# Fifteen small transfers of x between two K blocks of a decode kernel

## The chip, the cores and the metric

The kernel runs on one core of a Trainium2 chip. A core has a matrix engine (TensorE, PE in the profile, with its weight loads as PEld), a vector engine (VectorE, DVE), an activation engine (ScalarE, ACT), a general engine (GpSimd, POOL) and a synchronising engine (SyncE, SP), which here issues transfers. Sixteen DMA engines move data between HBM and the core's memory SBUF. The metric is the device time in microseconds, lower is better; a profile is taken of one execution and gives its span from the first to the last instruction.

## The reference

One token is decoded. x is one row of 1024 numbers. It is normalised, and two branches start from the result xn:

```
x = A_x
xn = layernorm(x)
out = x + A(xn, k_cache, v_cache, wq, wo) + B(xn, w1, w2, w3, w4)

A: q = xn @ wq                      # 32 query heads of 128
   scores = q . k * 128**-0.5       # 4 key/value heads, 8 query heads on each
   o = softmax(scores) . v          # 65536 cached positions
   return o @ wo
B: h = gelu(layernorm(xn) @ w1)     # w1, w2 are 1024 x 1024
   x1 = xn + shifted(h) @ w2        # four quarters of h, shifted by +1, -1, +2, -2
   return x1 + gelu(layernorm(x1) @ w3) @ w4      # w3 1024 x 3584, w4 3584 x 1024
```

All arrays are bf16. The K and V caches hold 4 heads x 65536 positions x 128 numbers each, 67 MB each; with the weights some 170 MB are read for one row of output.

## The kernel before

One large SBUF tile, KV, has 98304 bf16 columns on all 128 partitions. It holds two K slots of 16384 columns (4 MB each, offsets KOFF) and two V slots of 32768 columns (8 MB each, offsets VOFF), and later the weights. KV is the last tile to be declared; a tile "align" of 96 columns stands before it and is used by nothing.

The main loop goes over 32 blocks n of 8192 positions, eight for each key/value head. A K load brings two blocks, a V load brings four. For a block, VectorE transposes K in place (Ttr, L501), PE computes the scores (QK, L511), VectorE and PE find the running minimum (stats1, MB, stats2), ScalarE takes the exponential (EXP, L539), PE and VectorE transpose the probabilities (PTr, L547 and L549), PE multiplies them with V (PV, L557), and ScalarE and GpSimd add the result to the running sum (FLASH, L565 to L570). The transposition and the scores of the next block are worked on while this one is finished.

Each engine has a list of its own (class _Q) that it goes through in the order written. A transfer is added with _dma: first the waits for earlier readers and writers of its target (_deps), then the issue, whose end raises the semaphore of its channel by 16. SP's list is straight: all loads of wq, K, V and the later weights, then the store of the result. At the end of iteration n come

```
            if n % 2:
                issue_k((n + 3) // 2)
            if n % 4 == 1:
                issue_v((n + 3) // 4)
```

so after iteration 17 SP issues K load 10 (L341; it waits until QK of blocks 16 and 17 has read the slot) and V load 5 (L349), and the next thing on its list is K load 11, after iteration 19, which waits for QK of block 19. K load 11 is read by the transposition of block 22. SP has one queue; what it issues is carried out by the DMA engines in that order. ScalarE issues one transfer, the load of x at the start (L329), on a queue of its own.

After the loop come the weights of branch B, wo and w4. The last of w4 arrives in four parts, its products are added into OUT_ps (L460), VectorE copies them (L717), SP stores them as four rows (L718) and waits for that store (L719).

Of the kernel before, what the change touches and what calls it, by code (L numbers as in the profile page):

```python
# [6 lines left out]
BF = mybir.dt.bfloat16  # L7
# [113 lines left out]
def _deps(q, reads, writes):  # L121
    need = {}
    for b in reads:
        for s, v in b.w.items():
            need[s] = max(v, need.get(s, 0))
    for b in writes:

        for s, v in (list(b.r.items()) if b.r and b.whole else list(b.w.items()) + list(b.r.items())):
            if not (q.in_order and s is q.sem):
                need[s] = max(v, need.get(s, 0))  # L130
    for s, v in need.items():
        q.wait((s, v))


def _done(ev, reads, writes, partial=False):
    for b in reads:
        b.add_read(ev)
    for b in writes:
        if partial:
            b.add_write(ev)  # L140
        else:
            b.set_write(ev)


def _op(q, fn, reads=(), writes=(), partial=False, tick=True):
    _deps(q, reads, writes)
    ev = q.op(fn, tick)
    _done(ev, reads, writes, partial)
    return ev
# [17 lines left out]
def _dma(q, chan, fn, reads=(), writes=(), partial=False):  # L167
    _deps(q, reads, writes)
    chan.n += 1
    ev = q.dma(fn, chan.sem, 16 * chan.n)  # L170
    _done(ev, reads, writes, partial)
    return ev


def bass_parallel_sum__gqa_block_cached__mixer_s_mlp__decode_kernel(
# [13 lines left out]
    P = 128  # L189
# [18 lines left out]
    with ExitStack() as es:  # L208
        E = es.enter_context

        def sb(name, shape, dt):
            return E(nc.sbuf_tensor(name, shape, dt))
# [4 lines left out]
        def sem(name):  # L217
            return E(nc.semaphore(name))
# [42 lines left out]
        acc = sb("acc", [P, KT_D], F32)  # L261
        g_bf = sb("g_bf", [P, KT_D], BF)
        gh_bf = sb("gh_bf", [P, KT_F], BF)
        sb("align", [P, 96], BF)
        KV = sb("KV", [P, 98304], BF)
        KOFF, VOFF = (0, 16384), (32768, 65536)
        EPI = KV[:, 61440:65536].bitcast(F32)
# [24 lines left out]
        q_sp = _Q("sp", None)  # L292
# [5 lines left out]
        def chan(name):  # L298
            if name not in chans:
                chans[name] = _DmaChan(sem("d_" + name))  # L300
            return chans[name]
# [41 lines left out]
        def issue_v(j):  # L343
            if j >= NV:
                return
            h, nb = divmod(j, NV // HKV)
            src = A_v_cache[0, h, nb * 4 * SUB:(nb + 1) * 4 * SUB, :].rearrange("(p c) d -> p (c d)", p=P)
            sl = j % 2
            _dma(q_sp, chan("v%d" % sl), lambda e: e.dma_start(out=KV[:, VOFF[sl]:VOFF[sl] + 32768], in_=src), writes=[b_V[sl]])  # L349
# [142 lines left out]
        def Ttr(n, idx):  # L492
            if n >= NT:
                for ix in idx:
                    q_dve.op(lambda e, ix=ix: e.memset(spare[:, ix:ix + 1], 0.0))
                return
            s, half = (n // 2) % 2, n % 2
            for ix in idx:
                c = KOFF[s] // 2 + 4096 * half + 1024 * ix
                _deps(q_dve, [b_K[s][half]], [])  # L500
                ev = q_dve.op(lambda e, c=c: e.transpose(out=KV32[:, c:c + 1024], in_=KV32[:, c:c + 1024]))  # L501
                b_T[s][half].add_write(ev)

        def QK(n):
            s, half = (n // 2) % 2, n % 2
            fns = []
            for we in range(4):
                w_hi, e_ = divmod(we, 2)
                for cm in range(4):
                    mv = bass.AP(KV[:].tensor, KOFF[s] + half * 8192 + cm * 128 + w_hi * 64 + e_, [[kstep, P], [512, 16], [2, 32]])  # L510
                    fns.append(lambda e, we=we, cm=cm, mv=mv: e.matmul(  # L511
                        S_ps[32 * cm:32 * cm + 32, :], Ycur[:, we, :, :].rearrange("p a g -> p (a g)"), mv,
                        start=(we == 0), stop=(we == 3), tile_position=(0, 32 * cm)))
            _grp(q_pe, fns, reads=[b_T[s][half], b_Yc], writes=[b_S])

        def stats1(n):
            m = n % 2
            _op(q_dve, lambda e: e.reduce_max(mrow[:, m:m + 1], S_ps[:, :], axis=AX.X), reads=[b_S], writes=[b_mrow[m]])  # L518
            _op(q_dve, lambda e: e.tensor_tensor(out=Rm[:, m, :], in0=sel16[:, :], in1=mrow[:, m:m + 1].broadcast_to([P, 16]), op=ALU.mult),  # L519
                reads=[b_mrow[m], b_const], writes=[b_R[m]])  # L520

        def MB(n):
            m = n % 2
            _op(q_pe, lambda e: e.matmul(MB_ps[:, 0:16], Lmat[:, :], Rm[:, m, :], start=True, stop=True),  # L524
                reads=[b_R[m], b_const], writes=[b_MB])

        def stats2(n):
            _op(q_dve, lambda e: e.tensor_reduce(out=Bst[:, n % 4:n % 4 + 1], in_=MB_ps[:, 0:16], axis=AX.X, op=ALU.min),  # L528
                reads=[b_MB], writes=[b_Bcol[n % 4]])

        def EXP(n):
            m = n % 2
            ko = 1 - m
            cL = 513 * m
            if n % 4 == 0:
                q_dve.wait((s_b, n // 4 + 1))
            _op(q_dve, lambda e: e.tensor_tensor(out=brun[:, m:m + 1], in0=brun[:, ko:ko + 1], in1=Bst[:, n % 4:n % 4 + 1], op=ALU.min),  # L537
                reads=[b_brun[ko], b_Bcol[n % 4]], writes=[b_brun[m]])
            _op(q_act, lambda e: e.activation(p_sb[:, m, :], S_ps[:, :], ACTF.Exp, bias=brun[:, m:m + 1], scale=SCALE, accum_out=tmpO[:, cL:cL + 1]),  # L539
                reads=[b_S, b_brun[m]], writes=[b_p[m], b_tmpL[m]])  # L540
            _op(q_dve, lambda e: e.tensor_tensor(out=dd[:, m:m + 1], in0=brun[:, m:m + 1], in1=brun[:, ko:ko + 1], op=ALU.subtract),  # L541
                reads=[b_brun[ko], b_brun[m]], writes=[b_dd[m]])
            _op(q_act, lambda e: e.activation(ff[:, m:m + 1], dd[:, m:m + 1], ACTF.Exp), reads=[b_dd[m]], writes=[b_ff[m]])  # L543

        def PTr(n):
            m = n % 2
            _op(q_pe, lambda e: e.matmul(PT_ps[:, :], permR[:, :], p_sb[:, m, :], start=True, stop=True),  # L547
                reads=[b_p[m], b_const], writes=[b_PT])
            _op(q_dve, lambda e: e.transpose(out=pT_f[:, :], in_=PT_ps[:, :]), reads=[b_PT], writes=[b_pT])  # L549
# [37 lines left out]
        def load_at(c0, bufs, ch, w, r0, nrow):  # L587
            load_rows(KV[:, c0:c0 + nrow * w.shape[1]], bufs, ch, w, r0, nrow)
# [3 lines left out]
        for n in range(NT):  # L592
            if n % NSUB == 0:
                q_pe.mark(const_sems)
                q_pool.mark()
            if n % 4 == 0:
                q_act.mark()
            if n % 4 == 2:
                q_dve.mark(const_sems)
            if n == 0 or n % 4 == 2:  # L600
                Ttr(n, range(4))
            ahead = n + 1 if n % 4 != 1 else None
            if n % 4 != 1:
                QK(n)
            if ahead:
                Ttr(ahead, [0])
            stats1(n)
            MB(n)
            stats2(n)
            EXP(n)  # L610
            if ahead:
                Ttr(ahead, [1])
            PTr(n)
            if ahead:
                Ttr(ahead, [2, 3])
            if n % NSUB == NSUB - 1:
                head_switch(n // NSUB + 1)
            if n % 4 == 0:
                QK(n + 1)
            PV(n)  # L620
            FLASH(n)
            if n % NSUB == NSUB - 1:
                head_end(n // NSUB)
            if n % 2:
                issue_k((n + 3) // 2)
            if n % 4 == 1:
                issue_v((n + 3) // 4)
            if n == NT - 3:
                load_at(KOFF[0], b_K[0][:1] + b_T[0], "w1", B_w1, 0, 8)
                load_at(KOFF[0] + 8192, b_K[0][1:], "w2", B_w2, 0, 8)  # L630
                b_epi.r.update(b_V[0].r)
                load_at(VOFF[0], [b_V[0]], "w3", B_w3, 0, 8)
            if n == NT - 1:
                load_at(VOFF[1], [b_V[1]], "wo", A_wo, 0, 32)
                load_at(KOFF[1], b_K[1] + b_T[1], "w40", B_w4, 0, 16)
# [80 lines left out]
        out_rows(*w4_rows(3), last=True)  # L716
        _op(q_dve, lambda e: e.tensor_copy(orow, OUT_ps[:, 0:256]), reads=[b_OUT], writes=[b_p[0]])  # L717
        ev_out = _dma(q_sp, chan("out"), lambda e: e.dma_start(out=out[0, 0, :].rearrange("(j n) -> j n", j=4), in_=orow[0:97:32, :]), reads=[b_p[0]])  # L718
        q_sp.wait(ev_out)  # L719

        q_sp.emit(nc.sync)
# [32 lines left out]
```

## Time and profile before

| What | Value |
|---|---|
| Time, median of 3 runs | 400.83 us (400.39, 400.83, 400.88) |
| The profiled execution: time | 400.37 us |
| The profiled execution: span | 399.0 us |
| Mean granted TensorE clock | 0.622 |
| Busy: PE / DVE / POOL / ACT | 175.9 / 235.4 / 91.6 / 49.1 us |
| Moved by DMA | 169.98 MB in 4912 packets, mean 426 GB/s |
| Share of the chain of waits: DMA / DVE / PE | 57% / 18% / 13% |

The time is that of a whole execution; the span is shorter by what lies before the first and after the last instruction. Busy times overlap. A packet is one piece of a transfer on one DMA engine; the packets of 4 bytes are those that raise a semaphore. The chain of waits is followed back from the last instruction, at each step to whatever released it. In the timeline an issue on SP is given from the moment its waits are over; the transfer itself goes on after it.

### The profile page before, as it was taken

To read this page: it belongs to the slowest core of one execution; us is meant where nothing else is said; L and a number is where in the kernel's file an instruction comes from. 1 tells how busy PE (TensorE), PEld (TensorE's weight loads), DVE (VectorE), ACT (ScalarE), POOL (GpSimd) and SP (SyncE) were. 2 spreads that over 40 slices of the span, in tenths; PEclk is the share of its full clock that TensorE was granted. 3 is DMA by queue.
4 is the path that set the end of the run, shared out by engine and by line. 5 is a ranking of instruction groups with operands and counts; after the bars stand their busy time and mean duration, and the time that the engine had idled before them with its cause. 6 is when DMAs were issued, how large, how long until landed. Compare 5 with 4: busy or idle time off the path is not lost.

```text
span 399.0 us, 4487 instructions
## 1 busy us (share of the span) xinstructions
PE 175.9 (44%) x1456; PEld 53.1 (13%) x1456; DVE 235.4 (59%) x403; ACT 49.1 (12%) x132; POOL 91.6 (23%) x173
## 2 busy tenths in 40 slices
PE   0044244455254525442544464245426442572775
PEld 0022111111011101110111111011101110121322
DVE  0024756784688388728864886487657756635411
ACT  1000020111021101110201020111021120110000
POOL 6000012232135212230253021304331222251000
PEclk9997555555556656665655556656555655567699
DMA  8989999999999999999999999999999999999995
GB/s 355 486 368 473 416 418 424 434 429 443 470 422 394 447 440 420 427 447 466 427 407 434 440 420 440 434 466 427 411 430 440 434 434 406 456 459 421 419 409 247
DMA packets 4912, 169.98 MB, mean 426 GB/s; under 512 B 676, under 2 KB 680, under 8 KB 808
## 3 DMA queue, kind: packets, MB, share of 16 engines
q1 hardware_dynamic: 4760, 169.87, 98.7%
q8 instruction: 5, 0.08, 0.1%
q10 hardware_dynamic: 144, 0.00, 0.0%
q14 instruction: 3, 0.02, 0.0%
HBM read 169.87 MB, written 0.00 MB: 426 GB/s over the span
## 4 chain that ended last, share of the span: by engine, by line
DMA 57%; DVE 18%; PE 13%; issue 10%; ACT 1%; another core or an unknown queue 0%; POOL 0%; DVEq 0%; SPq 0%; ACTq 0%; POOLq 0%
DMA KV<-in_A_k_cache_dram 42%; DVE KV L501 13%; DMA KV<-in_B_w_dram 9%; PE S_ps L511 8%; DMA x_bf<-in_A_x_dram 6%; DVE mrow L518 2%; PE PT_ps L547 2%; PE OT_ps L557 1%; PE MM_ps L639 1%; ACT p_sb L539 1%; DVE pT_f L549 1%; PE MB_ps L524 1%; PE MM_ps L647 0%; DVE Rm L519 0%
## 5 line engine op out<-in xcount | busy, mean ns | idle before, releaser
L501 DVE STREAM_TRANSPOSE KV<-KV 128x1024 f32<-128x1024 f32 x128 | 149.5, 1211 | 23.9 <-DMA KV<-in_A_k_cache_dram 23.9
L511 PE MATMUL S_ps<-KV,Ycur 128*32 128x512 bf16 x512 | 59.5, 613 | 84.4 <-DVE KV L501 84.0
L570 POOL TENSOR_TENSOR O_acc<-O_acc,tmpO 128x513 f32<-128x513 f32 x32 | 40.8, 1275 | 121.9 <-ACT tmpO L565 121.9
L557 PE MATMUL OT_ps<-KV,pT_f 128*32 128x512 bf16 x512 | 58.9, 610 | 19.5 <-DVE pT_f L549 18.7
L518 DVE TENSOR_REDUCE mrow<-S_ps 128x1 f32<-128x512 f32 x32 | 22.1, 691 | 38.4 <-PE S_ps L511 38.4
L539 ACT ACTIVATE p_sb<-S_ps,brun 128x512 bf16<-128x512 f32 x32 | 22.0, 687 | 137.7 <-DVE brun L537 137.7
L547 PE MATMUL PT_ps<-p_sb,permR 128*128 128x512 bf16 x32 | 17.3, 541 | 44.5 <-ACT p_sb L539 44.5
L565 ACT ACTIVATE tmpO<-OT_ps 128x512 f32<-128x512 f32 x32 | 19.2, 599 | 136.8 <-PE OT_ps L557 78.3
L511 PEld LDWEIGHTS S_ps<-KV,Ycur 128*32 128x32 bf16 x512 | 14.4, 126 | 125.3 <-DVE KV L501 96.3
L549 DVE STREAM_TRANSPOSE pT_f<-PT_ps 128x512 f32<-128x512 f32 x32 | 22.7, 709 | 12.1 <-PE PT_ps L547 11.4
L567 POOL TENSOR_TENSOR spare<-ff 128x1 f32<-128x1 f32 x32 | 6.2, 193 | 102.0 <-ACT ff L543 100.3
L568 POOL TENSOR_SCALAR O_acc<-O_acc,ff 128x514 f32<-128x514 f32 x32 | 22.4, 701 | 0.0
L557 PEld LDWEIGHTS OT_ps<-KV,pT_f 128*32 128x32 bf16 x512 | 15.7, 130 | 50.6 <-DVE pT_f L549 28.9
L524 PE MATMUL MB_ps<-Rm,Lmat 128*128 128x16 bf16 x32 | 6.1, 191 | 25.3 <-DVE Rm L519 25.3
L528 DVE TENSOR_REDUCE Bst<-MB_ps 128x1 f32<-128x16 f32 x32 | 5.6, 174 | 14.2 <-PE MB_ps L524 14.2
L389 PE MATMUL MM_ps<-ln_s,ones_f 128*128 128x1 f32 x6 | 1.8, 362 | 27.0 <-DVE ln_s L388 27.0
L385 DVE CAST xT<-x_bf 128x8 f32<-128x8 bf16 x1 | 0.2, 170 | 21.3 <-DMA x_bf<-in_A_x_dram 21.3
L401 POOL TENSOR_TENSOR ln_s<-ln_s,neghalf 128x1 f32<-128x1 f32 x3 | 1.7, 558 | 40.5 <-DVE ln_s L399 40.5
L524 PEld LDWEIGHTS MB_ps<-Rm,Lmat 128*128 128x128 bf16 x32 | 3.3, 102 | 52.5 <-DVE Rm L519 52.5
L547 PEld LDWEIGHTS PT_ps<-p_sb,permR 128*128 128x128 bf16 x32 | 3.2, 101 | 47.3 <-ACT p_sb L539 47.3
L541 DVE TENSOR_TENSOR dd<-brun 128x1 f32<-128x1 f32 x32 | 5.7, 178 | 3.6
L537 DVE TENSOR_TENSOR brun<-brun,Bst 128x1 f32<-128x1 f32 x32 | 5.5, 172 | 3.7
(117 smaller groups left out, 123.4 us busy)
## 6 DMA issues: line engine op xcount, KB each, us to landing
KV<-in_A_k_cache_dram SPq DMA_DIRECT2D x16, 4096.0 KB, 23.7
KV<-in_B_w_dram SPq DMA_DIRECT2D x1, 7168.0 KB, 33.7
KV<-in_B_w_dram SPq DMA_DIRECT2D x2, 2048.0 KB, 15.1
KV<-in_B_w_dram SPq DMA_DIRECT2D x1, 4096.0 KB, 34.8
KV<-in_B_w_dram SPq DMA_DIRECT2D x1, 1536.0 KB, 34.0
KV<-in_B_w_dram SPq DMA_DIRECT2D x1, 1024.0 KB, 36.0
KV<-in_B_w_dram SPq DMA_DIRECT2D x1, 512.0 KB, 36.8
KV<-in_A_v_cache_dram SPq DMA_DIRECT2D x8, 36.1
```

Source lines behind the costliest of these rows:

```text
L501: ev = q_dve.op(lambda e, c=c: e.transpose(out=KV32[:, c:c + 1024], in_=KV32[:, c:c + 1024]))
L511: fns.append(lambda e, we=we, cm=cm, mv=mv: e.matmul(S_ps[32 * cm:32 * cm + 32, :], Ycur[:, we, :, :].rearrange("p a g -> p (a g)"), mv, s ...
L518: _op(q_dve, lambda e: e.reduce_max(mrow[:, m:m + 1], S_ps[:, :], axis=AX.X), reads=[b_S], writes=[b_mrow[m]])
L524: _op(q_pe, lambda e: e.matmul(MB_ps[:, 0:16], Lmat[:, :], Rm[:, m, :], start=True, stop=True), reads=[b_R[m], b_const], writes=[b_MB])
L539: _op(q_act, lambda e: e.activation(p_sb[:, m, :], S_ps[:, :], ACTF.Exp, bias=brun[:, m:m + 1], scale=SCALE, accum_out=tmpO[:, cL:cL + 1]) ...
L547: _op(q_pe, lambda e: e.matmul(PT_ps[:, :], permR[:, :], p_sb[:, m, :], start=True, stop=True), reads=[b_p[m], b_const], writes=[b_PT])
L549: _op(q_dve, lambda e: e.transpose(out=pT_f[:, :], in_=PT_ps[:, :]), reads=[b_PT], writes=[b_pT])
L557: fns.append(lambda e, q=q, q4=q4: e.matmul(OT_ps[32 * q4:32 * q4 + 32, :], pT_bf[:, q, :, 1], KV[:, v0 + 512 * q:v0 + 512 * (q + 1)], sta ...
L565: _op(q_act, lambda e: e.activation(tmpO[:, 1:513], OT_ps[:, :], ACTF.Copy), reads=[b_OT], writes=[b_tmpO])
L567: q_pool.op(lambda e: e.tensor_tensor(out=spare[:, 4:5], in0=ff[:, m:m + 1], in1=ff[:, m:m + 1], op=ALU.add), False)
L568: b_Oacc.set_write(q_pool.op(lambda e: e.tensor_scalar(out=O_acc[:, :], in0=O_acc[:, :], scalar1=ff[:, m:m + 1], scalar2=0.0, op0=ALU.mult ...
L570: ev = q_pool.op(lambda e: e.tensor_tensor(out=O_acc[:, m:m + 513], in0=O_acc[:, m:m + 513], in1=tmpO[:, m:m + 513], op=ALU.add), tick=(s_ ...
```

## The change

After K load 10 and V load 5 have been issued (n = 17), SP issues fifteen more transfers. The first copies 15 rows of 64 bytes (32 numbers each) from the start of x to partitions 0 to 14 of a new tile, the next copies 14 rows, and so on down to one row. Each has a column range of its own in the tile, none has a wait of its own, and all share one new semaphore. Nothing reads the tile. At the end SP waits for all of them before it waits for the store of the result. The tile "again" takes the place of "align": 15 x 32 columns instead of 96, so KV begins 768 bytes later on each partition.

```
-        sb("align", [P, 96], BF)
+        again = sb("again", [16, 15, 32], BF)
         KV = sb("KV", [P, 98304], BF)
...
             if n % 4 == 1:
                 issue_v((n + 3) // 4)
+            if n == 17:
+                rows = A_x[0, 0, :].rearrange("(a b) -> a b", b=32)
+                for k in range(15, 0, -1):
+                    ev_again = _dma(q_sp, chan("again"), lambda e, k=k: e.dma_start(out=again[0:k, k - 1, :], in_=rows[0:k, :]), writes=[_B()])
             if n == NT - 3:
...
         ev_out = _dma(q_sp, chan("out"), ...)
+        q_sp.wait(ev_again)
         q_sp.wait(ev_out)
```

More of the change, by code (lines that the diff above doesn't have):

```diff
@@ L263, in bass_parallel_sum__gqa_block_cached__mixer_s_mlp__decode_kernel @@
         gh_bf = sb("gh_bf", [P, KT_F], BF)
-        sb("align", [P, 96], BF)
+        again = sb("again", [16, 15, 32], BF)
         KV = sb("KV", [P, 98304], BF)
@@ L627, in bass_parallel_sum__gqa_block_cached__mixer_s_mlp__decode_kernel @@
                 issue_v((n + 3) // 4)
+            if n == 17:
+                rows = A_x[0, 0, :].rearrange("(a b) -> a b", b=32)
+                for k in range(15, 0, -1):
+                    ev_again = _dma(q_sp, chan("again"), lambda e, k=k: e.dma_start(out=again[0:k, k - 1, :], in_=rows[0:k, :]), writes=[_B()])
             if n == NT - 3:
@@ L718, in bass_parallel_sum__gqa_block_cached__mixer_s_mlp__decode_kernel @@
         ev_out = _dma(q_sp, chan("out"), lambda e: e.dma_start(out=out[0, 0, :].rearrange("(j n) -> j n", j=4), in_=orow[0:97:32, :]), reads=[b_p[0]])
+        q_sp.wait(ev_again)
         q_sp.wait(ev_out)
```

## The prediction

> **What bounds the kernel now.** I read the stretch table first, then the page's DMA rows, then SyncE's (SP's) timeline and waits, then the chain of waits.
>
> From the table by stretches (us, busy per engine, granted clock, DMA share, GB/s), two periods of four K/V blocks, the second of which receives the new transfers:
>
> ```profile
> core 0: us, PE busy (x) PEld busy (x) DVE busy (x) ACT busy (x) POOL busy (x), PEclk, DMA share, GB/s
> 193.70:232.30 38.60, 17.91 (x136) 4.63 (x136) 26.34 (x41) 5.80 (x16) 11.80 (x22) 0.53 1.00 435
> 232.30:271.00 38.70, 16.84 (x136) 4.51 (x136) 26.44 (x41) 5.80 (x16) 8.57 (x12) 0.59 1.00 434
> ```
>
> The 16 DMA engines are busy all the time, and the same 434 GB/s comes back in each period; VectorE, the busiest compute engine, works 26.4 of 38.7 us. The transfers bound this stage: time lost on their rings is lost, time lost on a compute engine mostly isn't.
>
> From the page, the packets by size and by queue (packets, MB, share of 16 engines):
>
> ```profile
> DMA packets 4912, 169.98 MB, mean 426 GB/s; under 512 B 676, under 2 KB 680, under 8 KB 808
> q1 hardware_dynamic: 4760, 169.87, 98.7%
> q10 hardware_dynamic: 144, 0.00, 0.0%
> ```
>
> Queue 10 is ScalarE's one load of x: 128 rows of 16 bytes and one semaphore packet on each of 16 engines, 144 in all. They show less than 0.05% of 16 x 399.0 us = 3.2 us, so under 22 ns for one tiny packet.
>
> SP's timeline (start us, us, issue), then its waits:
>
> ```profile
> 209.83 0.33 SPq L341 DMA_DIRECT2D KV<-in_A_k_cache_dram  x1
> 210.21 0.42 SPq L349 DMA_DIRECT2D KV<-in_A_v_cache_dram  x1
> 232.33 16.45 SPq L341 DMA_DIRECT2D KV<-in_A_k_cache_dram  x2
> ...
> 397.36 0.62 SPq L718 DMA_DIRECT2D out_dram<-p_sb  x1
> ```
>
> ```profile
> SPq L57 <- PE S_ps L511: 313.6, 15, 54.0
> SPq L57 <- DMA out_dram<-p_sb: 1.0, 1, 1.0
> ```
>
> 209.83 is K load 10, 210.21 is V load 5 (both at n = 17), 232.33 is K load 11 (n = 19). In between SP stands still for 21.70 us until QK has freed the K slot (it waits so for 313.6 us in all). The new issues fall into this gap.
>
> The chain of waits, with the K load that lies behind the new transfers, and the end:
>
> ```profile
> 232.33 23.78 DMA KV<-in_A_k_cache_dram
> ...
> 359.63 36.78 DMA KV<-in_B_w_dram
> 396.46 0.42 PE OUT_ps L460 x8
> 396.90 0.42 DVE p_sb L717
> ```
>
> K load 11 lands at 256.11. Its 4.19 MB at 434 GB/s need 9.7 us, so its bytes start moving at 246.4: for 14.1 us after its issue the rings still work on V load 5. And the last load ends the kernel, so a delay of the rings goes through to 396.4 and to the end.
>
> One thing no view prints: the trace keeps each DMA packet's start, duration and size, and I read those records too. A 32 KB packet starts 1.21 us after the one before it on its engine; with the 4-byte semaphore packet of a finished load between them it is up to 6 ns more, and a 16-byte packet of x, its load's semaphore packet and that of the other queue follow one another at 6 ns. The 16 semaphore packets of each bulk load are spread over 1.83 us, the same spread from 128 us to 357 us: eleven engines within the first 0.43 us, five at 0.73, 0.94, 1.32, 1.70 and 1.83. The spread grew when 16 KB and 8 KB instruction fetches (queues 8 and 14; those of 16 KB lasted 0.89 to 0.97 us) fell on single engines at 44, 55, 85 and 116 us. A load has landed when its latest engine is done.
>
> **The change part by part.**
>
> *Fifteen issues on SP.* A bulk issue takes 0.33 to 0.44 us, the only issue of fewer than 16 rows (the output, four) 0.62. Fifteen take 6.3 (at 0.42) to 9.3 us (at 0.62), nearest to the output's. They run from 210.63 to 217 or 220, under a wait that ends at 232.3: nothing on the path. Without that cover they would cost 6.3 to 9.3 us. The queue behind has two reserves, 12 us on SP and 14.1 us in the rings, so an issue would have to last 21.70/15 = 1.45 us before K load 11 is even issued later.
>
> *The packets.* The output makes one data packet and one semaphore packet for each of its four rows. By that row the fifteen transfers make 120 + 120 packets, on 15, 14 ... 1 engines. Spread evenly that is 15 for each engine; stacked, an engine that has a share in all fifteen gets 30. At 6 ns the 30 take 0.18 us, at the page's 22 ns 0.66 us. I take 6 ns, since those rows are the same size and stand back to back. Below nothing it cannot go: packets on a full ring only add. The upper end has one thing more: the records show three tiny packets in a row, not thirty, so the engine might run dry once while it fetches rows with nothing large ahead of them. The nearest row is the whole round trip of the output, 1.0 us. Together 0.18 to 1.66 us on the worst engine, 0.18 taken.
>
> [...]
>
> *Where it meets the spread.* Rings stay full to the end, so each engine keeps its lag. On one of the eleven early engines even 1.40 us (1.83 - 0.43) vanishes behind the latest. Only what falls on the late five can reach the end: nothing if the stack is on an early one, at most the full 0.18 to 1.66 us. Taken: 0.1 us, between nothing and 0.18, as I can't tell which engine is which.
>
> *KV moves.* In the program as built the tile "align" starts at byte 31552 and KV at 31744 = 31 x 1024. The new tile takes 960 bytes instead of 192, so KV starts at 32512 = 127 x 256. All loads write there. I take nothing: each packet is 4 to 64 KB. The trace has no load at such an offset. Low end nothing (a gain is excluded at 434 GB/s in every period); high end one extra piece per packet, priced as the output's 512-byte packet, 0.03 us, on about 264 packets per engine: 7.9 us.
>
> [...]
>
> *The second wait at the end* is passed 150 us earlier and stands ahead of the 1.0 us that SP waits for the output anyway: at most 0.03 us of issue, hidden; without that cover, the same 0.03.
>
> Sum: the profiled execution has span 399.0 and time 400.37, so 400.37 + 0.1 = 400.47. It is 0.46 below the median 400.83; set to the median, 400.9.
>
> **The rivals.**
>
> *B, the stack is on a late engine and runs dry.* 0.8 to 1.66 us reach the end: 401.6 to 402.5. For it: five of sixteen engines are late, and no long row of tiny packets is in the trace. Against: semaphore packets between loads make no gap.
>
> *C, SP is held because too many transfers are open.* The trace shows five bulk loads open at once (after 359.63), 45 packets per engine; here 17 are open before K load 11, with 18 + 30 packets. If the queue took 16, K load 11 could go out only after V load 5 has landed at about 246.4; an issue (0.4) and the way to the first packet (0.79 to 1.8 at the start, 1.0) leave the rings dry for 1.4 us. If it took 6, eleven small issues at 0.42 come first: 1.4 + 4.6 = 6.0 us. That gives 402.2 to 406.8. It decides once SP is held beyond 245. Against: no bulk issue ever lasts over 0.44 us, whatever is queued.
>
> *D, the shift of KV costs* up to 7.9 us, 4 in the middle: 401.6 to 408.7. Against: nothing in the trace; it is simply not shown.
>
> *E, each small transfer pays a round trip of its own on its engine.* Fifteen times the output's 1.0 us is 15 us, of which up to 1.83 are hidden: 414 to 416. Against it: a finished load and the next stand 6 ns apart on an engine. It is the one that a count of transfers, and not bytes, would give.
>
> [...]
>
> *F, the instruction fetches fall elsewhere.* SP's program grows. One more 16 KB fetch on a late engine adds up to 0.97 us (401.8); one that misses a late engine, or hits an early one instead, takes as much away (399.9).
>
> **How the numbers follow.** No measurable change, with a cost of nothing to 0.7 us: 0.55. B 0.15, C 0.09, D 0.06, E 0.03, F slower 0.05, F faster 0.07. A measurement of this kernel (400.39 to 400.88) can tell about 0.2%, 0.8 us, from no change. Faster 0.07, the same 0.55, slower 0.15 + 0.09 + 0.06 + 0.03 + 0.05 = 0.38. The likeliest case's own range is 400.4 to 401.6. For eight in ten I add B, F's upper side and the lower third of C and D, to 403.4, and the measurement's noise below, to 400.1; E, most of C and D, and F's gain are left out.
>
> **What would show it.** Packets under 512 B rise from 676 to about 916. Fifteen short issues follow 210.6, and K load 11 is still issued near 232.3; if that start moves to 246, C holds. Stretches stay at 1.00 and 434 GB/s; a drop in all of them is D, and a dip only at 244 to 256 is B or E. K load 11 lands within 0.2 us of 256.1, and the last B_w load ends near 396.4. The prediction is wrong if a long row of tiny packets is not as cheap as three of them, or if the late engine is the one that gets them all.

## The result, and the profile after

The changed kernel takes 402.00 us (median of six runs, 401.84 to 402.42) against 400.76 (six runs, 400.39 to 400.88). The medians are 1.24 us apart, and the ratio of the runs is 1.0034 with a 95% interval of 1.0023 to 1.0044: slower by more than the 0.2% that the prediction called measurable. The time lies in the stated range; the likeliest case, no measurable change, did not come. The profiled execution took 402.01 us, with a span of 400.8 instead of 399.0.

From the page of the changed kernel, the packets by size:

```profile
DMA packets 5152, 169.99 MB, mean 424 GB/s; under 512 B 916, under 2 KB 920, under 8 KB 1048
```

There are 240 more packets under 512 bytes, 120 rows and 120 semaphores, as counted beforehand. SP's timeline of the changed kernel (start us, us, issue):

```profile
210.26 0.33 SPq L341 DMA_DIRECT2D KV<-in_A_k_cache_dram  x1
210.63 0.43 SPq L349 DMA_DIRECT2D KV<-in_A_v_cache_dram  x1
211.11 5.40 SPq L631 DMA_DIRECT2D again<-in_A_x_dram  x15
232.30 16.71 SPq L341 DMA_DIRECT2D KV<-in_A_k_cache_dram  x2
```

The fifteen issues take 5.40 us, 0.36 each, and end at 216.5. K load 11 is issued at 232.30, as before (232.33). So nothing was lost on SP's queue.

The table by stretches (us, busy per engine, granted clock, DMA share, GB/s), and below it the chain of waits, both of the changed kernel:

```profile
193.70:232.30 38.60, 16.70 (x134) 4.65 (x136) 26.81 (x41) 5.80 (x16) 12.14 (x23) 0.54 1.00 431
232.30:271.00 38.70, 15.41 (x122) 4.32 (x128) 25.80 (x40) 5.80 (x16) 7.29 (x11) 0.50 1.00 424
271.00:309.70 38.70, 16.51 (x141) 4.64 (x139) 26.89 (x41) 5.81 (x16) 12.13 (x23) 0.54 1.00 434
```

```profile
232.30 25.38 DMA KV<-in_A_k_cache_dram
...
360.86 37.26 DMA KV<-in_B_w_dram
398.16 0.42 PE OUT_ps L460 x8
398.60 0.42 DVE p_sb L721
```

The stretch with the new transfers drops to 424 GB/s while the share still says 1.00: the records have twenty 32 KB packets begun between 244.47 and 247.52 that last 1.25 to 2.41 us instead of 1.21, and the share counts a packet as busy for as long as it lasts. The next stretch is back at 434. K load 11 lands at 257.68 instead of 256.11, 1.57 us later with the same issue time, and the last products start at 398.16 instead of 396.46, 1.70 us later. Nearly all of the loss is made at one place, between V load 5 and K load 11, and stays to the end; a last 0.1 us is added at 368 us, as told under F below.

The records of single packets say where. In this execution the sixteen engines finish K load 10 between 224.95 and 226.68, much as before (224.93 to 226.76); K load 11 they finish between 254.51 and 257.30, where before it was 253.93 to 255.76. So the latest finish has moved by 1.54 us, the earliest by 0.58. The two engines that finish last begin their packets of K load 11 at 247.37 and 247.63, over a microsecond after the last packet of V load 5 has ended on any engine (246.27).

### The profile page after: what moved, and what is told of

Its sections match the earlier page's. It is cut to its first block, busy times and chain, and to the rows that moved or that the text cites. A ratio compares the mean times of both kernels' runs of the same rounds, so it can differ in the third digit from the quotient of the medians.

```text
span 400.8 us, 4486 instructions
## 1 busy us (share of the span) xinstructions
PE 165.6 (41%) x1440; PEld 53.1 (13%) x1456; DVE 235.8 (59%) x403; ACT 49.1 (12%) x132; POOL 92.1 (23%) x173
## 4 chain that ended last, share of the span: by engine, by line
DMA 57%; DVE 21%; PE 12%; issue 8%; another core or an unknown queue 1%; DVEq 0%; POOL 0%; SPq 0%; ACT 0%; ACTq 0%; POOLq 0%
DMA KV<-in_A_k_cache_dram 42%; DVE KV L501 16%; DMA KV<-in_B_w_dram 9%; PE S_ps L511 9%; DMA x_bf<-in_A_x_dram 6%; DVE mrow L518 2%; PE OT_ps L557 1%; PE MM_ps L643 1%; DVE pT_f L549 1%; PE MB_ps L524 1%; PE MM_ps L651 0%; DVE Bst L528 0%; DVE Rm L519 0%; DVE brun L537 0%
## 5 line engine op out<-in xcount | busy, mean ns | idle before, releaser
L511 PE MATMUL S_ps<-KV,Ycur 128*32 128x512 bf16 x512 | 60.4, 621 | 104.2 <-DVE KV L501 103.9
L557 PE MATMUL OT_ps<-KV,pT_f 128*32 128x512 bf16 x512 | 57.3, 596 | 35.2 <-DVE pT_f L549 34.4
L547 PE MATMUL PT_ps<-p_sb,permR 128*128 128x512 bf16 x16 | 8.0, 499 | 21.7 <-ACT p_sb L539 21.7
L685 PE MATMUL S_ps<-KV,o_bf 128*1 128x512 bf16 x64 | 7.1, 379 | 1.8 <-DMA KV<-in_A_wo_dram 1.8
```

The lines of the kernel that those rows point to most:

```text
L511: fns.append(lambda e, we=we, cm=cm, mv=mv: e.matmul(S_ps[32 * cm:32 * cm + 32, :], Ycur[:, we, :, :].rearrange("p a g -> p (a g)"), mv, s ...
L557: fns.append(lambda e, q=q, q4=q4: e.matmul(OT_ps[32 * q4:32 * q4 + 32, :], pT_bf[:, q, :, 1], KV[:, v0 + 512 * q:v0 + 512 * (q + 1)], sta ...
L685: _grp(q_pe, [lambda e, lhs=lhs, rhs=rhs, jj=jj: e.matmul(S_ps[32 * jj:32 * jj + 1, :], lhs, rhs[:, 512 * jj:512 * jj + 512], start=False, ...
```

## The experiments

In all of them the tile "again" stays, so KV begins at byte 32512 as in the changed kernel. Times are medians; each is compared with runs of the kernel before made beside it.

### The tile alone

```
             if n == 17:
-                rows = ...
-                for k in range(15, 0, -1):
-                    ev_again = _dma(...)
...
-        q_sp.wait(ev_again)
```

> The larger tile stays, so KV begins at byte 32512 as in the changed kernel, and the fifteen transfers and the wait for them are taken out. Theory (an engine runs dry over its long row of tiny packets): 400.8, the time before, ratio 1.000. Rival D (the shift of KV costs): 402.0, ratio 1.003.

Measured: 400.62 against 400.55, ratio 1.0001 (0.9992 to 1.0010). The shift of KV by 768 bytes costs nothing measurable; rival D falls, and the loss belongs to the transfers.

### Fifteen transfers of one row

```
-  out=again[0:k, k - 1, :], in_=rows[0:k, :]
+  out=again[0:1, k - 1, :], in_=rows[0:1, :]
```

> Fifteen transfers as in the change, but each of one row: 15 data and 15 semaphore packets on one engine, none on the others. Theory: the engine with the longest row sets the loss, so nearly all of it stays, 401.5 to 402.3, and in the packet records one engine's lag grows by about 3 us behind V load 5 while fifteen keep theirs. Rival (the loss comes from fifteen engines being shifted against one another, or from the sum of 120 rows): at most a fifth of it, 400.8 to 401.0.

Measured: 400.84 against 400.55, ratio 1.0005 (0.9996 to 1.0014). The time missed what was expected, and the records bear out half of it: one engine is late and fifteen are not, but by 2 us and not by 3. That engine alone carries the fifteen transfers, one every 13 ns, from 244.54 to 244.74. Its next two packets are stretched, and those of the other fifteen engines are not:

```
packets of K load 11 on that engine, ns:   2389 1788 1213 1213 1213 1213 1213 1213
on each of the other fifteen:              1213 1213 1213 1213 1213 1213 1213 1213
```

With the 0.20 us of the row itself it is 1.95 us late. But it was 0.24 us behind the first engine when the latest was 1.75 behind, so only 0.44 us got past the latest. The chain of waits of this kernel has that amount: K load 11 lands at 256.56.

```profile
232.18 24.38 DMA KV<-in_A_k_cache_dram
```

### One transfer of 17 rows, and one of 31

```
-                for k in range(15, 0, -1):
-                    ev_again = _dma(... out=again[0:k, k - 1, :], in_=rows[0:k, :])
+                ev_again = _dma(... out=again[0:17, 0, :], in_=rows[0:17, :])
```

> [...] If the loss is paid per packet (each a read that the engine waits for), it stays: 401.5 to 402.5. If it is paid per transfer (its end and semaphore), it goes: 400.8. [...]

Measured: 400.50 against 400.55, ratio 1.0002 (0.9993 to 1.0011). The records show all 17 rows on one engine, as the forecast of a price per packet needs, 7 ns apart, and no stretched packet. As that left a choice between the number of packets (18 against 30) and the number of transfers, I then took 31 rows, with the tile made 31 partitions high:

> One transfer of 31 rows in place of the fifteen: 31 data packets and one semaphore packet on one engine, against 15 and 15 with fifteen transfers of one row and 17 and 1 with one of 17 rows. Theory (an engine reads ahead a limited number of packets, more than 18 and fewer than 30, and runs dry behind a longer row): that engine's next 32 KB packets take some 2.4 and 1.8 us instead of 1.21, its lag grows by about 1.9 us. Rival (the semaphores, or the number of transfers, make it run dry): lag grows by 0.2 us only. The time is 400.5 to 400.9 in both cases, since an early engine's 1.9 us is mostly hidden; the packet records decide.

Measured: 400.61 against 400.57, ratio 0.9999 (0.9989 to 1.0008). The page, SP's timeline and the chain of waits of the 31-row kernel, one line each:

```profile
DMA packets 4944, 169.98 MB, mean 426 GB/s; under 512 B 708, under 2 KB 712, under 8 KB 840
```

```profile
211.39 0.33 SPq L630 DMA_DIRECT2D again<-in_A_x_dram  x1
```

```profile
232.44 23.77 DMA KV<-in_A_k_cache_dram
```

The 32 more packets are 31 rows and one semaphore packet, where a bulk load has sixteen, one for each engine: the transfer ran on a single engine. Those 32 packets pass in 0.22 us, no later packet on any engine is stretched, and K load 11 lands 23.77 us after its issue, as before. My theory that a limited number of packets is read ahead falls: 32 packets with one semaphore cost nothing, 30 with fifteen cost 1.95 us. The price hangs on the transfer, not on the row.

### One transfer behind each load

```
             if n % 2:
                 issue_k((n + 3) // 2)
+                again_rows(n)        # the next of the fifteen, up to n = 27
             if n % 4 == 1:
                 issue_v((n + 3) // 4)
-            if n == 17: ... fifteen transfers
+            if n == 17:
+                again_rows(n)
```

> The same fifteen transfers, 15 rows to 1 row, but one behind each K load issued after n = 1 to 27 and one more behind V load 5, so each stands alone among bulk packets. Theory (the loss comes only from a row of tiny packets longer than the engine reads ahead): 400.8, ratio 1.000. Rival (each transfer costs its engine some 0.2 us wherever it stands, fifteen of them 3 us): 402.0, the time of the change.

Measured: 400.80 against 400.55, ratio 1.0006 (0.9997 to 1.0015). The chain of waits of this kernel:

```profile
232.44 23.75 DMA KV<-in_A_k_cache_dram
```

The same 120 rows and fifteen semaphores, one transfer at a time, leave K load 11 where it was. A transfer is not dear wherever it stands; a row of them is.

### Another place to read from, another to write to

The profiled execution of the changed kernel shows, besides stretched packets, some forty single rows 0.05 to 0.3 us apart instead of 13 ns, up to 247.6. I took them for fifteen engines holding each other up on 960 bytes of x. Two runs tested that:

```
-  in_=rows[0:k, :]
+  in_=A_k_cache[0, k % 4, 13 * k:13 * k + 4001 * (k - 1) + 1:4001, 0:32]
```

> The fifteen transfers with their shapes and targets, but the 64-byte rows come from the K cache, each row 1 MB from the next and another set for each transfer, instead of 120 reads of the same 960 bytes of x. Theory (the reads of one small place by fifteen engines at once hold each other up): the slow single packets, 0.13 to 0.23 us apart, go, every engine with a long row loses about 1.9 us and no more, and 0.2 to 0.6 us reach the end: 400.8 to 401.2. Rival (the place that is read doesn't matter): 402.0, with the slow singles.

```
-  again = sb("again", [16, 15, 32], BF)
+  again = sb("again", [P, 15, 32], BF)
-  out=again[0:k, k - 1, :]
+  out=again[0:8 * k - 7:8, k - 1, :]
```

> The fifteen transfers from x, but the rows go to partitions 0, 8, 16 and so on instead of 0 to 14. Theory (the reads hold each other up): no change against the changed kernel, 401.8 to 402.2, slow singles as there. Rival (fifteen engines writing to neighbouring partitions hold each other and the K and V writes up): 400.8 to 401.2, no slow singles.

Measured: far rows 401.95 against 400.57, ratio 1.0035 (1.0022 to 1.0047); far partitions 402.20, ratio 1.0041 (1.0026 to 1.0055). Neither place matters for the time. And the singles are absent in both profiled executions, though the second reads x exactly as the change does. So the loss doesn't need them, and the theory of the common place falls. In the profiled execution of the change they are part of it all the same: the two engines that finish K load 11 last carry nothing but small packets from the end of V load 5 to 247.37 and 247.63, and the eight large packets behind are not stretched. Singles of the same kind, rows that last 8 or 9 ns and not 11, come again with sixteen and with two rows (44 and 11 of them); when they come is open.

Without the singles the records can be read engine by engine, by the number of transfers that each carried:

```
far rows    transfers   lag behind the first engine   loss up to the end of K load 11, us
engine      15          0.00                          1.99
            14          0.41                          1.80
            13          0.71                          1.68
            12          1.27                          1.49
            10          1.76                          1.27  (ends at 256.92, the last of all)
            9           1.56                          1.11
            1           1.87                          0.01
            0           0.49                          0.00
```

The engines that are already late carry 12, 10, 9 and 1 transfers; those with 15 and 14 are early. K load 11 is held up not by the engine with the longest row but by late ones with a middling one.

### All engines alike

```
-  out=again[0:k, k - 1, :], in_=rows[0:k, :]
+  out=again[0:16, k - 1, :], in_=rows[0:16, :]
```

> Fifteen transfers of 16 rows each: 30 tiny packets on each of the 16 engines, so the late engines get them too. Theory (a late engine has nothing to hide behind): at least the 1.75 us that one engine lost by its two stretched packets comes through whole, and 240 reads of x instead of 120 hold each other up for longer: 402.5 to 405. Rival (the loss comes from the engines being treated unequally, 15 to 1 packets): 400.8.

Measured: 402.91 against 400.57, ratio 1.0056 (1.0039 to 1.0073), 2.3 us more, near the lower end of what was expected. Fifteen transfers on a late engine, with nothing to hide behind, cost their full two microseconds and a little more. The chain of waits (this execution took 403.21 us) has K load 11 landing at 258.92, 2.8 us later than before:

```profile
232.57 26.35 DMA KV<-in_A_k_cache_dram
```

### Two rows against four

```
-  out=again[0:k, k - 1, :], in_=rows[0:k, :]
+  out=again[0:2, k - 1, :], in_=rows[0:2, :]      # and 0:4 in the second
```

> Fifteen transfers of 2 rows each. Theory by now: a transfer, not a row, holds an engine's reading up by some 0.17 us; the first five or six behind a large packet are covered, fifteen lose 1.8 to 2.0 us; and the lag an engine already has decides what of it reaches the end. [...] So 2 rows hit early engines alone: 400.7 to 401.2. Rival (the number of rows in all, 30 of the change's 120, counts): 400.9, no help to tell by itself.

> [...] Theory: 1.0 to 1.3 plus 2.0 less the 1.8 of the latest, 1.2 to 1.5 us more than before: 401.7 to 402.1, the full cost of the change with 60 rows of its 120, and clearly more than with 2 rows. Rival (the cost goes with the number of rows): half of the change's, 401.2. Rival (which engine doesn't matter): the same as with 2 rows.

Measured: 2 rows 400.77 against 400.53, ratio 1.0008 (0.9999 to 1.0017); 4 rows 402.62, ratio 1.0058 (1.0044 to 1.0072). Both forecasts suppose, as my estimate, the engines of the far-rows table: for 2 rows those with 15 and 14 transfers, which lag 0.00 and 0.41 us, for 4 rows those with 15 to 12, the latest at 1.27 (1.0 to 1.3 in the forecast). With 2 rows the time alone can't tell the theory from its rival's 400.9. With 4 it lies above the 401.7 to 402.1 that was expected, and half of the change's rows cost more than the whole change, so the number of rows is out. The lines of the chain of waits, first 2 rows, then 4:

```profile
232.38 24.09 DMA KV<-in_A_k_cache_dram
```

```profile
232.40 24.96 DMA KV<-in_A_k_cache_dram
...
361.23 37.29 DMA KV<-in_B_w_dram
```

In the records of the 4-row run four engines with fifteen transfers each lose 1.96, 1.93, 1.84 and 1.95 us; they lagged 0.21, 0.26, 0.79 and 1.04 us, the latest of all 1.89. The worst comes to 1.04 + 1.95 = 2.99, which is 1.10 beyond the latest. At K load 11 that is the whole loss, just below the 1.2 to 1.5 expected. K load 11 lands at 257.36, so up to there 4 rows cost less than the change (257.68). The time says 2.1 us, and the rest arises later: between 360 and 381 us that same engine goes from a lag of 2.99 to 3.83, with a 64 KB packet stretched from 2.42 to 2.95 us just behind an 8 KB instruction fetch at 368.2. In the kernel before, an engine goes from 0.94 to 1.78 over the same fetch (at 366.1), and the latest stands at 1.83: the fetch was hidden there, and is paid once an engine has become the last.

### Twice as many, and half as many

```
-  for k in range(15, 0, -1): ... out=again[0:k, k - 1, :], in_=rows[0:k, :]
+  for k in range(30): ... out=again[k // 15:k // 15 + 1, k % 15, :], in_=rows[0:1, :]
```

> [...] Theory: fifteen more at 0.17 us each and all of it uncovered, 2.4 to 3.0 us on top of the 400.84 of fifteen: 403.2 to 403.9. Rival (an engine runs dry once, whatever the length of the row): 400.8 to 401.1.

```
-                for k in range(15, 0, -1):
+                for k in range(7, 0, -1):
```

> [...] Theory: the covered few, nothing reaches the end, 400.5 to 400.8. Rival (a third of the transfers' cost, 28 rows of 120 or 7 transfers of 15): 400.9 to 401.2.

Measured: thirty 403.70 against 400.53, ratio 1.0076 (1.0062 to 1.0090); seven 400.75, ratio 1.0007 (0.9998 to 1.0016). Both as expected. SP's timeline and the chain of waits with thirty:

```profile
211.18 11.36 SPq L631 DMA_DIRECT2D again<-in_A_x_dram  x30
```

```profile
232.42 26.77 DMA KV<-in_A_k_cache_dram
```

Still the issues end at 222.5, ten microseconds before K load 11 is issued at 232.42, but it lands at 259.19, 3.1 us later than before. On the one engine the first packet of K load 11 takes 4.69 us and the second 1.79, and the row itself takes 0.67 us, because a few packets late in it last some 0.15 us. With seven, the records give the short end of the scale. Put together, the loss of an engine by the number of transfers in its row:

```
transfers   us lost   from
3           0.04      seven to one
4           0.05      seven to one
5           0.06      seven to one
6           0.26      seven to one
7           0.46      seven to one
9           1.11      far rows
10          1.27      far rows
12          1.49      far rows
13          1.68      far rows
14          1.80      far rows
15          1.95      one row each
30          4.71      thirty
```

Up to five cost the 13 ns of their packets. From the sixth on each costs nearly 0.2 us: (1.95 - 0.06) / 10 = 0.19 and (4.71 - 1.95) / 15 = 0.18. The line is not straight in between: 9 and 10, both from late engines of the far-rows run, lie 0.3 us above it.

## Why the prediction was right or wrong

*The bound* held. The rings are full before and after (DMA share 1.00 in the stretches of both), SP's standstill up to 232.30 covered the issues, and what a late engine lost came out at the end: 1.57 us at K load 11, 1.70 at the last products.

*Fifteen issues on SP.* Right in kind: hidden, with 0.36 us each instead of 0.42 to 0.62, and K load 11 issued on time. Rival C, SP held by too many open transfers, did not occur even with thirty: 0.38 us each, and K load 11 issued at 232.42.

*The packets* is the step that failed. Their pace was right: the 15 + 15 packets pass in 0.20 us, against 0.18 worked out from 6 ns each. What was wrong is taking that pace for the price, with "run dry once", 1.0 us, as the upper end. The worst engine of the one-row run lost 1.95 us: 0.06 for the first five transfers and 0.19 for each one after them. It shows not in the tiny packets but in the two large ones behind them. The three tiny packets in a row that I had from the head of the trace lie within the five that are covered, so they could not show it.

*Where it meets the spread.* The idea was right and is the best-supported part: an engine's loss reaches the end only as far as it passes the latest one. It explains why 1.95 us became 0.3 with one row, 1.1 at K load 11 with four, and 2.3 with sixteen. The 0.2 to 0.3 us in the times with one row, with two rows, with seven transfers and with one behind each load are no more than noise allows (each interval includes no change); there only the records tell the cases apart. But I put the loss on "an early one" or "a late one" and left out the ramp's middle: engines with 9 to 12 transfers lose 1.1 to 1.5 us each, and three of the late five are among them.

*KV moves* and *the second wait*: nothing, as taken; the first is shown by the run with the tile alone, the second was not tried alone.

*The rivals.* B gave 401.6 to 402.5, and 402.00 lies in it; its outline, a loss on a late engine, is what happened, though its one round trip is not. So it is partly luck that the time lies in the range: its upper part was there for a loss of another price. E priced each transfer at 1.0 us in a row and is far off, but its form was right, a price for each transfer: 0.19 us, and the first five free. At its 1.0 us thirty in a row would have cost one engine 30 us; they cost 4.7. D and C fell. F came in another form: an 8 KB fetch comes at 366 to 368 us as before, but to an engine made late. In the change an engine goes from a lag of 2.05 us to 2.90 over the fetch at 367.8 and passes the latest at 2.79, which adds 0.11 us; in the far-rows run the engine with 12 transfers goes from 2.47 to 3.31, past 2.75, and in the 4-row run it is 0.84. The prediction said that each engine keeps its lag to the end, and had read the lags up to 357 us.

*What stays open.* Why the first five are free, and why 9 and 10 transfers lie 0.3 us above the line, no run shows: a record has a packet's start, duration and size, and nothing of what an engine does between two packets. Whether the price is that of a transfer's start or of its semaphore could not be told apart, since each transfer has one of each (fifteen transfers and fifteen semaphore packets in the one-row run).

## What to carry to other kernels

Look at the DMA engines one by one, not at their mean: K load 11 landed 0.4 us after the last packet of its latest engine (257.68 after 257.30; before, 256.11 after 255.76), so a cost on a late engine is paid in full (2.8 us there with 16 rows, on all engines alike), while 1.95 us on an early one came to 0.44 with one row. What is hidden now, like the 0.84 us of the fetch here, is paid once another delay has made its engine the last (0.11 us of it in the change). Count small transfers by transfer and not by row or byte, and, as far as these rows of 64 bytes go, don't queue more than about five in a row between large ones (five cost an engine 0.06 us, fifteen 1.95): one transfer of 31 rows, or fifteen spread out behind the loads, cost nothing measurable here (ratios 0.9999 and 1.0006). A price read off a few small packets in a row holds for a few.

## What the runs showed of the hardware

Fifteen one-row transfers on one engine pass at 13 ns each, yet the next 32 KB packet takes 2.39 us instead of 1.21 (4.69 behind thirty), and one more is stretched, to 1.79. The DMA share of such a stretch remains 1.00, so that the share alone hides the loss; the GB/s (424 against 434) and the landing time show it. The transfers of 17 and of 31 rows each ran on a single engine, with one semaphore packet. And after the instruction fetches of 8 and 16 KB between 44 and 116 us (0.31 and 0.89 to 0.97 us each, in the kernel before) single engines are up to 1.9 us behind; from 128 to 357 us the latest stays 1.83 us behind, while the DMA share is 1.00.
